# Hashed attention with a mixture of adapters: the shift to the head of each pair, the signs' read ahead of the crossbar transpose, the routing a slot earlier

## The chip, the core and the metric

The program runs on one core of one Trainium2 chip. The metric is device time in microseconds (us) of one execution. The core has five engines with a queue each: TensorE (PE in the profile; PEld is its weight loads), VectorE (DVE), ScalarE (ACT), GpSimd (POOL) and SyncE (SP). SP computes nothing here; it issues nearly all DMAs, in the order in which they are written.

## The reference, cut to what matters

```python
def _attn_ref(q, k, v, proj):            # 4 batches x 8 heads x 768 positions x 64
    q_bits = (np.einsum('bhsd,dk->bhsk', q, proj) > 0).astype(np.int64)   # 6 bits
    k_bits = (np.einsum('bhsd,dk->bhsk', k, proj) > 0).astype(np.int64)
    ...
    mask = q_bucket[:, :, :, None] == k_bucket[:, :, None, :]
    scores = np.where(mask, scale * np.matmul(q, k.transpose(0, 1, 3, 2)), -1000000000.0)
    ...
    return np.matmul(attn, v)            # attn: softmax over keys

def _moe_ref(x, w_gate, A, B):           # x 3072 x 512, 8 experts of rank 16
    logits = x @ w_gate
    topk = np.argpartition(-logits, K, axis=1)[:, :K]          # K = 2
    ...                                  # w: softmax over the two
    return x + sum(w[:, e] * (x @ A[e]) @ B[e])                # over the two chosen
```

A query sees only the keys whose six sign bits are its own. The attention's output goes, batch by batch, through a layer that picks two of eight low-rank adapters for each position.

## The kernel before, in words

The work is cut into 16 pairs of heads (pair p is batch p // 4, heads 2(p % 4) and the next; hp = p % 4). All data of a pair stays on the core. Each pair has nine slots. In slot s TensorE makes a block of 128 x 1024 scores (line 333) into one of three PSUM buffers, ScalarE turns it into weights with one exponential (line 340), two slots behind at most, and TensorE multiplies the weights with v (line 360) into the one bank `pv`, a head at a time; VectorE's `norm` (lines 378 and 380) divides and frees that bank.

The mask is part of the score's product: rows 64 to 70 of `aug` hold the signs of the hash beside the 64 rows of q or k, so that a score is only large where all six signs agree. `aug` has three buffers; that of pair p+2 is made while pair p runs:

- `natcast` (POOL, line 231, two casts) and `cross` (line 237), a DMA through the crossbar that writes q and k transposed, both heads on 128 rows;
- `shift` (line 246), which copies the second head's 64 rows down to rows 0 to 63, queries on VectorE, keys on POOL;
- `turn32` (DVE, line 189), `hash` (PE, line 199, in the bank `m`), `sign` (line 208 on DVE, line 211 on POOL), `sign_out` (line 217), a DMA of the signs to DRAM, and `sign_in` (line 223), a DMA of them back into rows 64 to 71 of `aug`. It overwrites what the crossing left there, so it follows the shift, which reads those rows.

The bank `m` is a single PSUM buffer. Its tenants, in order: the hash, `turn` (x transposed on PE, line 398, copied by DVE, line 399), the logits `lgz` (line 412) until `route2` (lines 441 and 445) has read them, `zt` (line 457) and `delta` (line 465, added to x by DVE, line 475). ScalarE's share in the routing is one small exponential (line 430), which stands between the big ones.

There is no scheduler: the program is recorded as `slot(p, s)` is written, and each engine runs its own instructions in that order. What is written early in a slot stands early in all five queues. SP is a queue like the others: a DMA that waits for its data holds up those behind it.

Of the kernel before, what the change touches and what calls it, by code (L numbers as in the profile page):

```python
# [19 lines left out]
class Emitter:  # L20
# [614 lines left out]
    def moe0(self, p):
        b, hp = p // self.PPB - 1, p % self.PPB
        if b >= 0 and hp == 2:
            self.route2(b, self.G0)
        if 0 <= b < self.B - 2 and hp == 3:
            self.route2(b, self.G1)  # L640
# [30 lines left out]
    def moe_last(self, p, s, b, hp):  # L671
        G0, G1 = self.G0, self.G1
        if hp == 2:
            if s == 2:
# [12 lines left out]
        if hp == 3:
            if s < 5:
                self.delta(b, s + 1)
            if s in (2, 4):  # L690
                self.store(b, s // 2, None, self.nc.sync)
            if s == 0:
                self.store(b, 0, None, self.nc.sync)
            if s == 1:
                self.turn(self.N - 3)
# [165 lines left out]
```

## Time and profile before

| what | value |
|---|---|
| time, median of 2 runs | 204.72 us (204.09 to 205.34) |
| the profiled execution | 207.21 us |
| its span, first to last instruction | 205.4 us |
| mean granted TensorE clock | 0.914 |
| busy: PE, ACT, POOL, DVE | 81%, 71%, 56%, 51% |

The profiled execution is a run of its own, 1.2% above the median of the others; the span is what its trace covers. No engine is busy throughout, so what has to be read is which engine waits for what in each pair.

### The profile page before, as it was taken

The page shows a single profiled execution, that of the slowest core. Times are in us where ns is not written, and L with a number is a line of the kernel's source. Part 1 is how long each engine was busy: PE and PEld are TensorE (multiplying, and loading weights), DVE is VectorE, ACT ScalarE, POOL GpSimd, SP SyncE. Part 2 cuts the span into 40 slices and gives each one's busy share as a digit, 9 for nine tenths or more (in the row PEclk, how much of TensorE's full clock was granted, in tenths as well). Part 3 has the DMA queues.
Part 4 walks back from the last instruction along what each step waited for, and adds up shares of the span by engine and source line. Part 5 has one row for each costly group of instructions (what it writes and reads, how often), then busy time and mean ns, then how long its engine had stood idle before and what let it go on. Part 6 is the DMA issues. An engine that isn't in the chain of part 4 may idle for free.

```text
span 205.4 us, 5316 instructions
## 1 busy us (share of the span) xinstructions
PE 166.1 (81%) x2158; PEld 112.0 (55%) x2159; DVE 105.4 (51%) x310; ACT 146.1 (71%) x168; POOL 115.9 (56%) x174
## 2 busy tenths in 40 slices
PE   7994984697989598989894998989986989698530
PEld 4642653365666366667562676656554767477310
DVE  1474084034253354756764537484946446766560
ACT  2168495368899687979994578899983878976340
POOL 7348489719499919296958055669593343011250
PEclk9999799679799979999999599999997999999975
DMA  5965599774949945747399919694699030142016
GB/s 117 293 131 163 116 333 192 136 202 52 304 73 290 288 82 142 181 107 221 94 279 217 268 23 288 134 258 81 206 213 268 13 112 3 45 167 109 3 62 246
DMA packets 61009, 33.44 MB, mean 163 GB/s; under 512 B 47416, under 2 KB 59192, under 8 KB 60984
## 3 DMA queue, kind: packets, MB, share of 16 engines
q1 hardware_dynamic: 59112, 32.17, 63.2%
q10 hardware_dynamic: 1744, 0.92, 1.5%
q8 instruction: 17, 0.28, 0.6%
q14 instruction: 8, 0.07, 0.1%
q0 software_dynamic: 128, 0.01, 0.0%
HBM read 20.16 MB, written 7.03 MB: 132 GB/s over the span
## 4 chain that ended last, share of the span: by engine, by line
POOL 28%; PE 27%; DMA 16%; issue 13%; DVE 10%; ACT 1%; POOLq 1%; SPq 0%
PE s L333 10%; DMA aug<-dr 9%; PE pv L360 6%; POOL nb L231 5%; POOL vs L179 4%; POOL xb L389 4%; POOL aug L246 4%; POOL vb L177 3%; POOL s L211 3%; DMA vn<-in_v_dram 3%; DVE acc L475 2%; DMA aug<-nb 2%; DMA dr<-s 2%; POOL vs L181 2%; POOL vb L182 2%
## 5 line engine op out<-in xcount | busy, mean ns | idle before, releaser
L340 ACT ACTIVATE P<-s 128x1024 bf16<-128x1024 f32 x144 | 138.5, 1034 | 35.6 <-PE s L333 26.8
L333 PE MATMUL s<-aug 71*128 71x256 bf16 (+2 forms) x384 | 86.7, 335 | 17.2 <-DMA aug<-dr 14.6
L360 PEld LDWEIGHTS <-P 128*128 128x128 bf16 x1080 | 51.5, 103 | 19.0 <-issue 6.9
L360 PE MATMUL pv<-vb,P 128*128 128x65 bf16 x1080 | 54.4, 201 | 0.0
L333 PEld LDWEIGHTS <-aug 71*128 71x128 bf16 x384 | 31.5, 101 | 37.0 <-issue 14.1
L389 POOL CAST xb<-x 128x768 bf16<-128x768 f32 x15 | 13.7, 910 | 58.3 <-DVE x L380 58.2
L189 DVE STREAM_TRANSPOSE R<-nat 128x768 f32<-128x768 f32 x30 | 27.7, 954 | 1.3 <-DMA nat<-in_k_dram 0.9
L231 POOL CAST nb<-nat 128x768 bf16<-128x768 f32 x30 | 24.0, 826 | 1.9 <-DMA nat<-in_q_dram 1.8
L399 DVE COPY xT<-xtp 128x768 bf16<-128x768 bf16 x15 | 8.4, 558 | 26.8 <-PE xtp L398 26.7
L475 DVE SCALAR_TENSOR_TENSOR acc<-dl,rt,x 128x512 f32<-128x512 f32 x21 | 15.6, 748 | 9.3 <-PE dl L465 9.3
L380 DVE TENSOR_TENSOR x<-pv,ri 128x384 f32<-128x384 f32 x30 | 16.7, 557 | 1.0
L179 POOL TENSOR_TENSOR vs<-vn 128x384 f32<-128x384 f32 x16 | 15.9, 995 | 0.0
L211 POOL TENSOR_SCALAR s<-sg,ssc 128x192 bf16<-128x192 bf16 x15 | 11.5, 763 | 5.8 <-DVE sg L208 5.1
L199 PE MATMUL hs<-R,hst 128*32 128x192 f32 x240 | 13.2, 338 | 0.6 <-DVE xT L399 0.6
L346 PE MATMUL pv<-vb,eps 128*128 128x390 bf16 x30 | 11.2, 372 | 3.2 <-POOL vb L182 2.6
L177 POOL CAST vb<-vn 128x768 bf16<-128x768 f32 x16 | 13.3, 830 | 0.6 <-DMA vn<-in_v_dram 0.5
L378 DVE RECIPROCAL ri<-pv 128x6 f32<-128x6 f32 x30 | 5.7, 191 | 15.1 <-PE pv L360 14.7
L246 POOL COPY aug<-aug 64x768 bf16<-64x768 bf16 x15 | 12.5, 830 | 1.7 <-DMA aug<-nb 0.9
L465 PE MATMUL dl<-Bcat,zT 128*128 128x512 bf16 x23 | 8.9, 403 | 3.0 <-DVE acc L475 1.9
L421 DVE MAX8 top<-lz 128x8 f32<-128x8 f32 x24 | 2.7, 163 | 16.1 <-PE lz L412 16.1
L199 PEld LDWEIGHTS hs<-R,hst 128*32 128x32 f32 x240 | 6.5, 111 | 8.0 <-DVE ri L378 2.5
L412 PE MATMUL lz<-wa,xT 128*128 128x136 bf16 x96 | 8.6, 222 | 2.4 <-ACT xT L743 2.1
(83 smaller groups left out, 137.6 us busy)
## 6 DMA issues: line engine op xcount, KB each, us to landing
vn<-in_v_dram SPq DMA_DIRECT2D x16, 384.0 KB, 5.1
nat<-in_q_dram SPq DMA_DIRECT2D x15, 384.0 KB, 5.3
nat<-in_k_dram SPq DMA_DIRECT2D x15, 384.0 KB, 4.9
out_dram<-acc SPq DMA_DIRECT2D x10, 512.0 KB, 3.4
dr<-s SPq DMA_DIRECT2D x15, 48.0 KB, 3.6
aug<-dr SPq DMA_DIRECT2D x15, 48.0 KB
out_dram<-acc SPq DMA_DIRECT2D x2, 256.0 KB, 4.9
out_dram<-acc ACTq DMA_DIRECT2D x1, 512.0 KB
```

Source lines behind the costliest of these rows:

```text
L177: nc.gpsimd.tensor_copy(out=vb[:, :, 0:T, 0:D], in_=vn)
L179: nc.gpsimd.tensor_add(out=s3, in0=vn[:, :, 0:3, :], in1=vn[:, :, 3:6, :])
L189: self.nc.vector.transpose(out=self.R[p][:, i], in_=self.nat[p][:, i])
L199: nc.tensor.matmul(out=self.hs[p][32 * j:32 * j + 32], lhsT=self.hst[:, hf].rearrange("p b i -> p (b i)"), rhs=rhs, start=(hf == 0), stop= ...
L211: nc.gpsimd.tensor_scalar(out=s2, in0=sg, scalar1=self.ssc, scalar2=None, op0=ALU.mult)
L231: self.nc.gpsimd.tensor_copy(out=self.nb[p][:, :, i].rearrange("p t h d -> p h t d"), in_=self.nat[p][:, i].rearrange("p h (t d) -> p h t ...
L246: eng.tensor_copy(out=aug[0:64, :, i, 1, :], in_=aug[64:128, :, i, 0, :])
L333: nc.tensor.matmul(out=ps[:, c - lo:c - lo + n * P], lhsT=aug[0:71, kt, 1, h, :], rhs=aug[0:71, q:q + n, 0, h, :], start=True, stop=True)
L340: self.nc.scalar.activation(out=self.P_[p][:, lo:lo + 1024], in_=ps, func=ACT.Exp, scale=128.0 if p == 0 else 0.125)
L360: self.nc.tensor.matmul(out=pv[:, i, :], lhsT=self.P_[p][:, o:o + P], rhs=vb[:, h, kt, :], start=False, stop=(kt == T - 1), skip_group_che ...
L389: self.nc.gpsimd.tensor_copy(out=self.xb[p], in_=self.x[b][:, :, hp * P:(hp + 1) * P])
L475: nc.vector.scalar_tensor_tensor(out=acc, in0=ps, scalar=rt, in1=x, op0=ALU.mult, op1=ALU.add)
```

## The change

`shift(p+1)` moves from slot 3 or 4 of pair p to its slot 0, on both engines. `sign_in(p+1)` moves from slot 5 to slot 0 and thereby ahead of `cross(p+2)` and of the loads of q and k in SP's queue; only the load of v stays in front of it. The loads of q and k now follow the crossing. The second half of `sign` goes from POOL to VectorE. The logits of a group of three blocks move from slots 6 and 7 to 5 and 6, their exponential from slot 8 to 7, `route2` from the next pair's slot 0 to slot 8. `turn` moves from slots 6, 0, 3, 6 (by hp) to slot 0 of every pair from 2 on. Both `zt` stand in hp 3, four of the six `delta` in slots 5 to 8 of hp 0. The stores of finished rows move from slot 0 to 6. In pair 1 the work for pair 3 stands one slot earlier. At the start there are 21 idle matmuls in three places, in place of 13 in one, and the load of v for pair 1 follows the signs' write.

```diff
@@ sign
-        nc.gpsimd.tensor_scalar(out=s2, in0=sg, scalar1=self.ssc, scalar2=None, op0=ALU.mult)
+        nc.vector.tensor_scalar(out=s2, in0=sg, scalar1=self.ssc, scalar2=None, op0=ALU.mult)
@@ start
-        for i in range(13):
-            nc.tensor.matmul(out=B[:, 0, 0:256], lhsT=self.wz[:, 0:128], rhs=self.wz, start=True, stop=True)
+        def busy(n):
+            for i in range(n):
+                nc.tensor.matmul(out=B[:, 0, 0:256], lhsT=self.wz[:, 0:128], rhs=self.wz, start=True, stop=True)
+
+        busy(16)
         self.T1(0, 0, tm)
         self.tcopy(0, 0, tm, "act")
+        busy(2)
         self.T1(1, 0, tv)
         self.tcopy(1, 0, tv, "act")
+        busy(3)
@@ slot
-        off = 4 if p == 0 else 1 if p == 1 else 0
-        if s == 0:
-            self.moe0(p)
-        if s == 3 + (p == 1) and p and hp < 2:
+        if s == 0 and p:
             self.shift(p + 1)
+        off = 4 if p == 0 else 0
+        if s == 0 and 2 <= p < N:
+            self.turn(p - 2)
         if s - off in (1, 2):
             self.turn32(p + 2, s - off - 1)
...
-        if s == 4 and hp >= 2:
-            self.shift(p + 1)
-        if s - off == 4:
+        late = {0: 8, 1: 5}.get(p, 4)
+        if s == late:
             self.hash(p + 2)
-        if s - off == (4 if p == 0 else 5):
+        if s == min(late + 1, 8):
             self.sign(p + 2)
...
         if s == 0 and p:
-            self.stores(p)
+            self.loadv(p + 2)
+            self.sign_in(p + 1)
+        if s - off == 1:
+            self.cross(p + 2)
+        if s == (6 if p == 0 else 1):
             self.loadqk(p + 3, 0)
             self.loadqk(p + 3, 1)
-            self.loadv(p + 2)
-        if s - off == 1:
-            self.cross(p + 2)
...
-        if s == 5 and p:
-            self.sign_in(p + 1)
-        if s - off == (4 if p == 0 else 5):
+        if s == min(late + 1, 8):
             self.sign_out(p + 2)
+        if s == 6:
+            self.stores(p)
@@ moe
-        if b >= 0 and L and s in (6, 7):
-            for i in (L[0:1], L[1:3])[s - 6]:
+        if L and s in (5, 6):
+            for i in (L[0:1], L[1:3])[s - 5]:
                 self.lgz(b, L, i)
-            if s == 7:
+            if s == 6:
                 self.route1(b, L)
-        if b >= 0 and hp == 3 and s == 5:
-            self.zt(b, G0)
-        if b >= 1 and hp == 0 and s == 2:
-            self.zt(b - 1, G1)
-        D = {(3, 7): 0, (3, 8): 1, (0, 0): 2, (0, 7): 3, (0, 8): 4, (1, 2): 5}.get((hp, s))
+        if L and s == 8:
+            self.route2(b, L)
+        if hp == 3 and s in (5, 6):
+            self.zt(b, (G0, G1)[s - 5])
+        D = {(3, 7): 0, (3, 8): 1, (0, 5): 2, (0, 6): 3, (0, 7): 4, (0, 8): 5}.get((hp, s))
```

In the last two pairs the routing of batch 2 moves likewise: `turn(13)` from slot 1 to slot 0 of pair 15, and `delta(1)` from pair 15 into pair 14.

**SP in pair 8.** Its DMAs before, from the store to the signs' write (the number behind `nat`, `vn`, `nb`, `aug` and `dr` begins with the pair or buffer; `s210` are the signs of pair 10):

```order
L483 DMA out_0_dram<-acc0_0_1684 128x1024
L161 DMA nat11_1716<-in_q_dram 128x2x384
L161 DMA nat11_1716<-in_k_dram 128x2x384
L169 DMA vn10_1719<-in_v_dram 128x2x384
L237 DMA_TRANSPOSE aug1_128<-nb10_1713 128x12x128
L223 DMA aug0_127<-dr9_1645 8x24x128
L217 DMA dr10_1834<-s210_1831 128x6x32
```

The same pair now:

```order
L169 DMA vn10_1735<-in_v_dram 128x2x384
L223 DMA aug0_127<-dr9_1661 8x24x128
L237 DMA_TRANSPOSE aug1_128<-nb10_1733 128x12x128
L161 DMA nat11_1760<-in_q_dram 128x2x384
L161 DMA nat11_1760<-in_k_dram 128x2x384
L217 DMA dr10_1849<-s210_1843 128x6x32
L483 DMA out_0_dram<-acc0_0_1698 128x1024
```

The read of pair 9's signs (line 223) went ahead of the crossing and of two of the three loads; the store went last.

**VectorE in pair 1.** Before, from the signs of pair 2 to the second `norm` of pair 0:

```order
L208 TENSOR_SCALAR sg2_388<-hs2_379 128x192
L378 RECIPROCAL ri0_0_442<-pv0_0_349 128x6
L380 TENSOR_TENSOR x0_440<-pv0_0_349,ri0_0_442 128x6x64
L189 STREAM_TRANSPOSE R3_445<-nat3_334 128x768 x2
L246 COPY aug2_129<-aug2_129 64x6x128
L378 RECIPROCAL ri0_1_510<-pv0_1_460 128x6
```

The same place now:

```order
L208 TENSOR_SCALAR sg2_396<-hs2_387 128x192
L211 TENSOR_SCALAR s22_398<-sg2_396,ssc_203 128x192
L246 COPY aug2_129<-aug2_129 64x6x128
L189 STREAM_TRANSPOSE R3_437<-nat3_342 128x768
L378 RECIPROCAL ri0_0_457<-pv0_0_357 128x6
L380 TENSOR_TENSOR x0_455<-pv0_0_357,ri0_0_457 128x6x64
L189 STREAM_TRANSPOSE R3_437<-nat3_342 128x768
L378 RECIPROCAL ri0_1_519<-pv0_1_472 128x6
```

The shift of pair 2 and the first transpose of pair 3 (which waits for the load `nat3`) now stand ahead of the `norm` of pair 0.

**VectorE from the end of pair 8 to the head of pair 9.** Before (`dl0_4` and `dl0_5` are two of the deltas of batch 0, `xtp7` is x of pair 7 transposed):

```order
L475 SCALAR_TENSOR_TENSOR acc0_2_1887<-dl0_4_1885,rt0_3_1523,x0_440 128x512
L378 RECIPROCAL ri8_0_1897<-pv8_0_1815 128x6
L380 TENSOR_TENSOR x2_1895<-pv8_0_1815,ri8_0_1897 128x6x64
L399 COPY xT1_1115<-xtp7_1900 128x768
L189 STREAM_TRANSPOSE R11_1934<-nat11_1716 128x768 x2
L475 SCALAR_TENSOR_TENSOR acc0_2_1887<-dl0_5_1956,rt0_3_1523,x0_440 128x512
L246 COPY aug1_128<-aug1_128 64x6x128
```

Now:

```order
L475 SCALAR_TENSOR_TENSOR acc0_1_1847<-dl0_2_1845,rt0_0_1319,x0_455 128x512
L475 SCALAR_TENSOR_TENSOR acc0_1_1847<-dl0_3_1868,rt0_3_1522,x0_455 128x512
L475 SCALAR_TENSOR_TENSOR acc0_2_1884<-dl0_4_1882,rt0_3_1522,x0_455 128x512
L475 SCALAR_TENSOR_TENSOR acc0_2_1884<-dl0_5_1897,rt0_3_1522,x0_455 128x512
L378 RECIPROCAL ri8_0_1908<-pv8_0_1827 128x6
L380 TENSOR_TENSOR x2_1906<-pv8_0_1827,ri8_0_1908 128x6x64
L246 COPY aug1_128<-aug1_128 64x6x128
L399 COPY xT1_1123<-xtp7_1913 128x768
L189 STREAM_TRANSPOSE R11_1944<-nat11_1760 128x768 x2
```

Four deltas now stand in a row in pair 8, and the shift stands ahead of the copy of xT and of the transposes.

## Rows read from the trace of the kernel before

**Rows 1.** Waits: engine, line, waited for; us in total, times, longest.

```profile
ACT P L340 <- PE s L333: 26.8, 35, 5.0
PE s L333 <- DMA aug<-dr: 14.6, 8, 4.7
```

**Rows 2.** Timeline of ACT: start, us, instruction, idle before and its releaser.

```profile
38.74 1.94 ACT L340 ACTIVATE P<-s 128x1024 bf16<-128x1024 f32 x2 [5.02 <-PE s L333]
...
113.39 1.02 ACT L340 ACTIVATE P<-s 128x1024 bf16<-128x1024 f32 x1 [3.33 <-PE s L333]
...
124.22 0.22 ACT L430 ACTIVATE e<-d 128x24 f32<-128x24 f32 x1 [1.24 <-DVE d L423]
...
180.69 2.05 ACT L340 ACTIVATE P<-s 128x1024 bf16<-128x1024 f32 x2 [1.29 <-PE s L333]
```

**Rows 3.** Windows by pairs: length; PE, PEld, DVE, ACT, POOL busy; clock; DMA; GB/s.

```profile
24.49:38.74 14.25, 8.94 (x132) 5.73 (x129) 6.86 (x12) 8.61 (x9) 13.29 (x18) 0.94 1.05 219
38.74:60.74 22.00, 19.90 (x242) 13.53 (x241) 7.68 (x17) 17.68 (x18) 13.05 (x22) 0.80 0.68 161
60.74:82.45 21.71, 18.52 (x261) 12.80 (x260) 10.16 (x33) 17.30 (x20) 16.33 (x24) 0.92 0.82 203
...
100.61:126.16 25.55, 21.77 (x267) 14.32 (x267) 14.54 (x41) 18.06 (x19) 14.56 (x21) 0.87 0.86 208
126.16:144.33 18.17, 17.04 (x255) 11.78 (x252) 11.37 (x34) 16.81 (x21) 12.24 (x16) 1.00 0.70 166
144.33:168.10 23.77, 20.19 (x267) 13.39 (x267) 14.43 (x40) 17.94 (x19) 12.98 (x19) 0.93 0.74 175
168.10:189.42 21.32, 18.41 (x296) 14.41 (x292) 12.81 (x44) 17.56 (x21) 3.11 (x5) 1.00 0.20 78
```

**Rows 4.** Timeline at the head of pair 9, SP and PE.

```profile
106.72 0.35 SPq L223 DMA_DIRECT2D aug<-dr  x1
...
112.26 1.03 PE L333 MATMUL s<-aug 71*128 71x512 bf16 x3 [2.48 <-DMA aug<-dr]
```

**Rows 5.** Chain that ended last: start, us, what.

```profile
12.13 4.09 DMA aug<-nb
...
47.37 2.45 DMA aug<-dr
...
106.72 5.50 DMA aug<-dr
```

**Rows 6.** Tile `aug`: crossing's issue and the shift, ns min/median/max; the DMAs' landing.

```profile
L237 SPq DMA_TRANSPOSE aug<-nb x15: 1426/2692/3422, 12.1 to 154.0; - x15
...
L246 DVE COPY aug<-aug x15: 356/356/721, 16.2 to 171.9; 64x768 bf16<-64x768 bf16 x15
L246 POOL COPY aug<-aug x15: 821/826/923, 16.4 to 173.0; 64x768 bf16<-64x768 bf16 x15
...
DMA to landing us min/median/max: 6.0/7.0/8.0
```

**Rows 7.** The page's costliest groups: busy us, mean ns of one, idle before.

```profile
L231 POOL CAST nb<-nat 128x768 bf16<-128x768 f32 x30 | 24.0, 826 | 1.9 <-DMA nat<-in_q_dram 1.8
...
L380 DVE TENSOR_TENSOR x<-pv,ri 128x384 f32<-128x384 f32 x30 | 16.7, 557 | 1.0
```

**Rows 8.** The page's DMA issues: KB each, median us to landing.

```profile
dr<-s SPq DMA_DIRECT2D x15, 48.0 KB, 3.6
```

**Rows 9.** Timeline of pair 1, PE and DVE.

```profile
26.76 0.34 PE L346 MATMUL pv<-vb,eps 128*128 128x390 bf16 x1 [0.45 <-DVE x L380]
...
26.99 2.03 DVE L189 STREAM_TRANSPOSE R<-nat 128x768 f32<-128x768 f32 x2 [0.29 <-DMA nat<-in_q_dram]
```

**Rows 10.** Timeline of PE in pair 12, the third of three deltas.

```profile
144.64 0.38 PE L465 MATMUL dl<-Bcat,zT 128*128 128x512 bf16 x1 [0.41 <-DVE acc L475]
```

**Rows 11.** Timeline of PE at the start.

```profile
1.04 2.95 PE L505 MATMUL hb<-wz 128*128 128x256 bf16 x13 [1.04 <-DVE wz L71]
...
5.93 2.93 PE L274 MATMUL ha<-qkT,projW 128*128 128x384 f32 x4
```

More of the change, by code (lines that the diff above doesn't have):

```diff
@@ L531, in first @@
             self.loadqk(2, 1)
-            self.loadv(1)
             self.cast(0, 1)
@@ L542, in first @@
             self.sign_out(1)
+            self.loadv(1)
             self.sign_here(0, 1, self.hc)
@@ L575, in slot @@
             self.norm(p - 1, 0)
-        off = 4 if p == 0 else 1 if p == 1 else 0
-        if s == 0:
-            self.moe0(p)
-        if s == 3 + (p == 1) and p and hp < 2:
+        if s == 0 and p:
             self.shift(p + 1)
+        off = 4 if p == 0 else 0
+        if s == 0 and 2 <= p < N:
+            self.turn(p - 2)
         if s - off in (1, 2):
             self.turn32(p + 2, s - off - 1)
-        if s == 4 + (p == 1):
+        if s == (5 if p == 1 else 4):
             self.norm(p - 1, 1)
             self.to_bf(p - 1)
-        if s == 4 and hp >= 2:
-            self.shift(p + 1)
-        if s - off == 4:
+        late = {0: 8, 1: 5}.get(p, 4)
+        if s == late:
             self.hash(p + 2)
-        if s - off == (4 if p == 0 else 5):
+        if s == min(late + 1, 8):
             self.sign(p + 2)
@@ L601, in slot @@
         if s == 0 and p:
-            self.stores(p)
+            self.loadv(p + 2)
[3 more added lines that the diff above has]
+        if s == (6 if p == 0 else 1):
             self.loadqk(p + 3, 0)
             self.loadqk(p + 3, 1)
-            self.loadv(p + 2)
-        if s - off == 1:
-            self.cross(p + 2)
         if p == 0 and s == 6:
-            self.loadqk(3, 0)
-            self.loadqk(3, 1)
             self.loadv(2)
-        if s == 5 and p:
-            self.sign_in(p + 1)
-        if s - off == (4 if p == 0 else 5):
+        if s == min(late + 1, 8):
             self.sign_out(p + 2)
+        if s == 6:
+            self.stores(p)
         if p in (1, 2, 3) and s in (6, 7):
@@ L626, in route_exps @@
             return
-        if s == 8 and hp == 1:
+        if s == 7 and hp == 1:
             self.route_exp(b, self.G0)
         if b == self.B - 2:
-            if hp == 2 and s == 6:
+            if hp == 2 and s == 4:
                 self.route_exp(b, self.G1)
-        elif s == 8 and hp == 2:
+        elif s == 7 and hp == 2:
             self.route_exp(b, self.G1)
[L635 to L640, printed above, removed]
     def stores(self, p):
@@ L650, in moe @@
         G0, G1 = self.G0, self.G1
-        if p < self.N - 1 and s == (6, 0, 3, 6)[hp] and p >= 2:
-            self.turn(p - 2)
+        if b < 0:
+            return
         if b == self.B - 2 and hp >= 2:
@@ L655, in moe @@
         L = {1: G0, 2: G1}.get(hp)
-        if b >= 0 and L and s in (6, 7):
-            for i in (L[0:1], L[1:3])[s - 6]:
+        if L and s in (5, 6):
+            for i in (L[0:1], L[1:3])[s - 5]:
                 self.lgz(b, L, i)
-            if s == 7:
+            if s == 6:
                 self.route1(b, L)
-        if b >= 0 and hp == 3 and s == 5:
-            self.zt(b, G0)
-        if b >= 1 and hp == 0 and s == 2:
-            self.zt(b - 1, G1)
-        D = {(3, 7): 0, (3, 8): 1, (0, 0): 2, (0, 7): 3, (0, 8): 4, (1, 2): 5}.get((hp, s))
-        if hp < 2:
+        if L and s == 8:
[3 more added lines that the diff above has]
+        D = {(3, 7): 0, (3, 8): 1, (0, 5): 2, (0, 6): 3, (0, 7): 4, (0, 8): 5}.get((hp, s))
+        if hp == 0:
             b -= 1
@@ L673, in moe_last @@
         if hp == 2:
-            if s == 2:
+            if s == 1:
                 self.zt(b, G0)
-            if s in (4, 5):
-                for i in (G1[0:2], G1[2:3])[s - 4]:
+            if s in (2, 3):
+                for i in (G1[0:2], G1[2:3])[s - 2]:
                     self.lgz(b, G1, i)
+            if s == 3:
+                self.route1(b, G1)
             if s == 5:
-                self.route1(b, G1)
+                self.route2(b, G1)
             if s == 6:
-                self.route2(b, G1)
-            if s == 7:
                 self.zt(b, G1)
-            if s == 8:
-                self.delta(b, 0)
+            if s in (7, 8):
+                self.delta(b, s - 7)
         if hp == 3:
-            if s < 5:
+            if s in (1, 2, 3, 4):
                 self.delta(b, s + 1)
[L690 to L695, printed above, removed]
+            if s in (0, 3, 5):
+                self.store(b, (0, 3, 5).index(s), None, self.nc.sync)
     def pv3(self, u, parts, where=None):
```

## The prediction

> **What bounds the kernel now.** I read the waits first. ScalarE's exponentials are the one long, even stream (144 of them), and they waited 26.8 us for scores; TensorE in turn waited 14.6 us, eight times, for the DMA that brings a pair's signs into `aug` [rows 1]. ACT's timeline then says where: the gaps sit at the heads of pairs, 5.02 us ahead of pair 2, 3.33 us ahead of pair 9, and shorter ones of the same kind ahead of pairs 5 and 13 [rows 2]. The windows, two pairs each, show what such a gap costs in all. Pairs 10 and 11 have none: 18.17 us, clock 1.00, PE busy 17.0 and ACT 16.8 of them (pairs 6 and 7 repeat it). Pairs 2 and 3, 4 and 5, 8 and 9, 12 and 13 have one each: 22.00, 21.71, 25.55 and 23.77 us, at a granted clock of 0.80 to 0.93 [rows 3]. So a gap is paid twice: while TensorE stands, and behind it, when part of the stretch runs at 1.2 instead of 2.4 GHz and PE, already as full as ACT, cannot keep up. A pair without a gap is bound by PE and ACT together, near 9.1 us.
>
> Why the signs are late can be read at pair 9. SP issues the read at 106.72, late in pair 8, and the read takes 5.50 us to land because crossing and loads are in front of it; TensorE starts the pair at 112.26, after 2.48 us of standing [rows 4, 5]. With little in front, a read lands 2.45 us after its issue [rows 5].
>
> **The read's new place (the main term).** The shift of pair p+1 now needs only its crossing, issued in slot 1 of the pair before, and the read follows right behind the shift, about 1.2 us into the pair (a `norm` and a copy on VectorE). Even at 5.50 us it is there at 6.7, before the 9.1 us are over; at 2.45 us there are some 5 us to spare. The gap goes, unless the read cannot be issued: it waits for its own signs' write. That is a loop through SP: read's issue 0.35 us [rows 4], crossing's issue 2.69 [rows 6], the issue of two loads (I put 0.65 each, nearly twice the read's), the signs' write 3.6 to landing [rows 8]: 7.9 us a pair, under 9.1. A second loop goes through POOL: crossing, shift 0.83 [rows 6], two casts of 0.83 [rows 7], next crossing. The crossing took 4.09 us early in the program [rows 5] and 6.0 to 8.0 behind loads [rows 6]. Now the loads come after it, so I take a value near 4.09: 6.6 us a pair; with 7.0 it would be 9.5. Both loops fit, the second not at all values.
>
> What is late next is then PE and ACT themselves, that is, the quiet pairs' time. Two pairs without routing (2 and 3) lack one wait of the routing, 1.24 us [rows 2], against 18.2, and I leave them some 0.5 for the first crossings: 17.5, a gain of 4.5. Pairs 4 and 5: 18.2, a gain of 3.5. Pairs 8 and 9, 12 and 13 also carry the deltas, below.
>
> **Deltas in a row.** Each delta and each `turn` wants the single bank `m` when VectorE has just been given it; the third of three deltas waited 0.41 us for the one before [rows 10]. Four deltas now stand in slots 5 to 8 of hp 0, and the `turn` of hp 1 behind them: four such waits, 1.6 us, on a PE that has nothing to spare. Pairs 8 and 9, and 12 and 13: 18.2 + 1.6 = 19.8, gains of 5.7 and 4.0. The bounds are 0 (if ACT's two slots of lead hide the waits) and 3.2.
>
> **Pair 1.** The gap of 5.02 us at its end goes: the signs of pair 2 need no shift late in pair 1 any more, and their read is not behind pair 3's crossing. But here the change adds a wait. VectorE's `norm` of pair 0, which frees the bank `pv`, now stands behind the first transpose of pair 3, and that waits for a load which landed at 26.99 [rows 9]. Queued behind it on VectorE is the `norm`, and TensorE waits for that with all of pair 1 behind it. TensorE had the bank at 26.76, after 0.45 us of waiting [rows 9]; now a transpose (half of 2.03 us) and a `norm` (0.56 [rows 7] and its short reciprocal, some 0.75) lie between 26.99 and its start: about 28.75, 2.0 us later. Whether so long a stand lowers the clock is open; after the stands of pairs 2, 5, 9 and 13 it did [rows 3], so I add 0.9, bounds 0 and 1.7. Pair 1 gains 5.0 - 2.0 - 0.9 = 2.1.
>
> **Routing, and the last pairs.** Logits, exponential and `route2` move by the same slot, so ACT's wait of 1.24 us for the logits [rows 2] stays: the hash still lies just ahead of them on PE. I cost it at nothing, bounds -0.6 and +0.3 for each of six. In pair 15 a delta and the `turn` cost ACT 1.29 us [rows 2]; one delta goes to pair 14 (0.4 there): a gain of 0.9.
>
> **The start.** Eight more idle matmuls. The 13 took 2.95 us, 0.21 each from start to start [rows 11]; the three added ahead end before the first transposes can start, the five between are at worst 1.1 us on the path. The four hash matmuls took 2.93 us at 1.2 GHz [rows 11]; if the fuller engine gets its clock before them, they take half, and 0.5 to 1 is won. I take 0.
>
> **POOL to VectorE.** 15 multiplications of some 0.36 us, the row of VectorE's copy [rows 6]; VectorE is busy 11.4 of 18.2 us in the quiet pairs [rows 3], and nobody waits for signs within a pair. 0, and 5.4 with no cover.
>
> **The sum** against the profiled execution: 2.1 + 4.5 + 3.5 + 5.7 + 4.0 + 0.9 = 20.7 of 205.4 us of span, so 184.7; the same off the median of 204.72 gives **184.0 us**. With the bounds of the terms, 180 to 190.
>
> **The rivals.**
>
> *The crossing still lands late (0.10).* For it: seven microseconds is its median [rows 6]. Then POOL and VectorE, which now have the shift first in a pair, stand at the head of every pair until it lands. At 8.0 a pair takes 8.0 + 0.83 + 1.66 = 10.5; fourteen of them 147, against 132 in my sum (17.5 + 18.2 x 3 + 19.8 x 2 + 20.4): 199. Against it: the 8.0 were behind three loads and a store.
>
> *Slower: the read misses every pair's start (0.05).* The read waits in SP for its signs' write, which now lies behind two loads that lie behind the crossing. With 3.42 us for the crossing's issue and 5.5 us for the write instead of 3.6, the loop is 0.35 + 3.42 + 1.3 + 5.5 = 10.6, over the 9.1 from which it decides. Before, four heads stood; now fourteen would, each at what pairs 4 and 5 paid, 3.5: 184 + 49 = 233.
>
> *The first pairs do not follow (0.12).* Pairs 1 to 3 depend on the first loads, at a DMA share of 1.05 of the engines' time in pair 1 [rows 3], not on the order. Without 2.1 and 4.5: 190.6.
>
> *The two halves of the shift hold each other up (0.03).* They now run side by side at each head. One copy of 15 on VectorE took 0.72 us instead of 0.36 [rows 6]; in its timeline a cast of POOL runs beside it. If each shift and no cover: 15 x 0.36 = 5.4, so 189.4. The Trainium skill, SBUF — State Buffer, "Who interferes with whom", says so in general: a VectorE copy in a two-port mode and a GpSimd instruction shut each other out for the whole of whichever began first. By that rule the one late copy is no accident, and the shift would last 0.36 + 0.83 at worst. The row agrees in part (0.72, not 1.19).
>
> *Better (0.10).* The deltas' waits are hidden (3.2) and half of the routing's waits go (3.7): 177.
>
> **How the numbers follow.** My forecast has 0.60, and 184.0 is its time. A measurement of this kernel can tell about 2% (200.6 to 208.8) from no change. Faster takes in the forecast, the first-pairs rival, the shift rival, the better one and half of the late crossing: 0.60 + 0.12 + 0.03 + 0.10 + 0.04 = 0.89; same is the rest of the late crossing, 0.06; slower 0.05. From 177 to 197 only the slower rival, half of the late crossings and half of the better case stay out, 0.15.
>
> **What the profile would show.** Right: no wait of TensorE for `aug<-dr` from pair 3 on, granted clock 1.00 from pair 4 to 15, quiet pairs of 18 us in all windows, PE waiting near 0.4 us for `acc` in hp 0, a stand of about 2.4 us for the `norm` in pair 1, ACT still waiting 1.2 us for the logits. Wrong: VectorE or POOL idle at pairs' heads for `aug<-nb`, SP waiting long for `dr<-s`, or a new wait of PE for the bank `m` that lasts over a microsecond and takes the clock with it.

## The result, and the profile after

The changed kernel takes 187.44 us (187.00 and 187.89, two runs) against 204.72: a ratio of 0.916, interval 0.900 to 0.931. Run again beside the kernel before, it took 185.77 us (183.61 to 187.44, six runs), ratio 0.909 (0.902 to 0.916). The prediction was 184.0, range 177 to 197. The profiled execution took 187.89 us, its span is 186.1 us, its mean granted clock 0.951. The profiled executions of the changed kernel and of runs 1, 2, 5 and 6 are the longest of their kernels' runs and that of run 4 is the shortest of its, so their rows are read for the place of a wait and not for a total.

The waits of the changed kernel (engine, line, waited for; us in total, times, longest):

```profile
POOL aug L246 <- DMA aug<-nb: 22.5, 13, 5.0
...
ACT P L340 <- PE s L333: 10.9, 23, 2.5
ACT e L430 <- DVE d L423: 10.1, 9, 1.8
...
PE pv L346 <- POOL vb L182: 4.3, 1, 4.3
```

TensorE's wait for `aug<-dr`, 14.6 us before [rows 1], has no row any more, and ScalarE waits 10.9 instead of 26.8 us. POOL now stands 22.5 us for the crossing, in front of its half of the shift, and only the first of these stands, 5.03 us, has a wait of TensorE behind it (below).

Its windows: pair 0, pair 1, then two pairs each, cut at the first exponential of a pair as in [rows 3]:

```profile
9.00:24.89 15.89, 10.62 (x129) 5.60 (x124) 6.85 (x12) 8.78 (x10) 10.14 (x15) 0.89 0.59 149
24.89:38.03 13.14, 11.04 (x138) 7.09 (x135) 5.30 (x11) 8.61 (x9) 8.49 (x11) 0.74 0.85 227
38.03:54.84 16.81, 16.79 (x245) 11.25 (x243) 11.04 (x23) 16.62 (x19) 11.72 (x20) 1.00 1.05 210
54.84:72.56 17.72, 17.08 (x259) 11.99 (x257) 11.71 (x36) 16.75 (x21) 13.41 (x20) 1.00 1.07 234
72.56:90.17 17.61, 16.73 (x252) 11.68 (x249) 12.24 (x35) 16.64 (x20) 12.30 (x17) 1.00 0.74 192
90.17:111.54 21.37, 19.55 (x270) 13.16 (x270) 16.18 (x43) 17.74 (x20) 12.66 (x18) 1.00 0.83 205
111.54:129.15 17.61, 16.73 (x252) 11.68 (x249) 11.92 (x35) 16.64 (x21) 11.71 (x16) 1.00 0.90 225
129.15:150.08 20.93, 19.17 (x270) 12.99 (x270) 15.63 (x43) 17.74 (x20) 13.22 (x19) 1.00 0.71 155
150.08:170.06 19.98, 17.87 (x290) 14.14 (x286) 12.10 (x42) 17.48 (x21) 2.26 (x5) 1.00 0.28 109
```

The clock, the third number from the end, is 1.00 in all pairs from 2 to 15. Pair 1 has 0.74: the only stretch at half clock that costs much now lies there. The gains by stretch, against [rows 3] and the starts of the exponentials in the two traces:

| stretch | before | after | gain | predicted |
|---|---|---|---|---|
| to the first exponential | 10.61 | 9.00 | 1.6 | 0 |
| pair 0 | 13.88 | 15.89 | -2.0 | 0 |
| pair 1 | 14.25 | 13.14 | 1.1 | 2.1 |
| pairs 2, 3 | 22.00 | 16.81 | 5.2 | 4.5 |
| pairs 4, 5 | 21.71 | 17.72 | 4.0 | 3.5 |
| pairs 6, 7 and 10, 11 | 36.3 | 35.22 | 1.1 | 0 |
| pairs 8, 9 | 25.55 | 21.37 | 4.2 | 5.7 |
| pairs 12, 13 | 23.77 | 20.93 | 2.8 | 4.0 |
| pairs 14, 15 | 21.32 | 19.98 | 1.3 | 0.9 |
| sum of the span | | | 19.3 | 20.7 |

Three places are left where time stands. The first two are in pairs 0 and 1; PE's timeline there (start, us, instruction, idle before and its releaser):

```profile
20.49 0.33 PE L346 MATMUL pv<-vb,eps 128*128 128x390 bf16 x1 [4.25 <-POOL vb L182]
...
28.81 0.51 PE L346 MATMUL pv<-vb,eps 128*128 128x390 bf16 x1 [2.10 <-DVE x L380]
```

What is in front of the two releasers on their engines, POOL and VectorE:

```profile
16.60 0.92 POOL L246 COPY aug<-aug 64x768 bf16<-64x768 bf16 x1 [5.03 <-DMA aug<-nb]
17.59 0.83 POOL L177 CAST vb<-vn 128x768 bf16<-128x768 f32 x1
```

```profile
27.11 0.98 DVE L189 STREAM_TRANSPOSE R<-nat 128x768 f32<-128x768 f32 x1 [0.99 <-DMA nat<-in_q_dram]
28.20 0.56 DVE L380 TENSOR_TENSOR x<-pv,ri 128x384 f32<-128x384 f32 x1
```

POOL stands 5.03 us in the shift of pair 1, with the cast of v for pair 0 behind it. VectorE waits for a load of pair 3 with the `norm` of pair 0 behind it. Both are stands of the order: what the engine waits for is not what TensorE needs. The third place is the row of deltas in pair 8, read from ACT's timeline:

```profile
97.82 1.02 ACT L340 ACTIVATE P<-s 128x1024 bf16<-128x1024 f32 x1 [0.19 <-PE s L333]
99.04 1.02 ACT L340 ACTIVATE P<-s 128x1024 bf16<-128x1024 f32 x1 [0.20 <-PE s L333]
100.32 1.02 ACT L340 ACTIVATE P<-s 128x1024 bf16<-128x1024 f32 x1 [0.26 <-PE s L333]
...
108.70 0.22 ACT L430 ACTIVATE e<-d 128x24 f32<-128x24 f32 x1 [1.60 <-DVE d L423]
```

The exponentials start 1.22 to 1.28 us apart there, against 0.91 in a quiet pair (8.19 us for nine in pair 7). The last row is the wait for the logits, which stays as it was.

### The profile page after: what moved, and what is told of

Same layout as the page of the kernel before. It is cut to its first block, busy times and chain, and to the rows that moved or that the text cites. A ratio compares the mean times of both kernels' runs of the same rounds, so it can differ in the third digit from the quotient of the medians.

```text
span 186.1 us, 5336 instructions
## 1 busy us (share of the span) xinstructions
PE 157.9 (85%) x2166; PEld 107.3 (58%) x2167; DVE 112.9 (61%) x325; ACT 143.6 (77%) x168; POOL 105.7 (57%) x159
## 4 chain that ended last, share of the span: by engine, by line
PE 29%; DMA 27%; POOL 16%; ACT 11%; DVE 6%; issue 5%; SPq 2%; POOLq 1%
DMA nat<-in_q_dram 17%; PE s L333 10%; ACT P L340 10%; DMA aug<-nb 9%; POOL nb L231 7%; PE pv L360 7%; PE hs L199 3%; POOL vs L179 3%; POOL vb L177 3%; DVE acc L475 2%; SPq L237 2%; PE dl L465 2%; DMA nat<-in_k_dram 2%; PE lz L412 2%; PE xtp L398 2%
## 5 line engine op out<-in xcount | busy, mean ns | idle before, releaser
L340 ACT ACTIVATE P<-s 128x1024 bf16<-128x1024 f32 x144 | 136.1, 1054 | 19.3 <-PE s L333 10.9
L333 PE MATMUL s<-aug 71*128 71x256 bf16 (+2 forms) x384 | 82.1, 320 | 2.9 <-ACT P L340 2.8
L360 PEld LDWEIGHTS <-P 128*128 128x128 bf16 x1080 | 48.0, 99 | 18.1 <-issue 5.6
L360 PE MATMUL pv<-vb,P 128*128 128x65 bf16 x1080 | 51.1, 196 | 0.0
L231 POOL CAST nb<-nat 128x768 bf16<-128x768 f32 x30 | 24.9, 831 | 11.2 <-DMA nat<-in_q_dram 7.9
L246 POOL COPY aug<-aug 64x768 bf16<-64x768 bf16 x15 | 12.6, 837 | 24.9 <-DMA aug<-nb 22.5
L389 POOL CAST xb<-x 128x768 bf16<-128x768 f32 x15 | 12.3, 822 | 23.4 <-DVE x L380 23.4
L346 PE MATMUL pv<-vb,eps 128*128 128x390 bf16 x30 | 10.2, 339 | 6.8 <-POOL vb L182 4.3
L199 PE MATMUL hs<-R,hst 128*32 128x192 f32 x240 | 15.9, 359 | 0.1
L208 DVE TENSOR_SCALAR sg<-hs 128x192 bf16<-128x192 f32 x15 | 5.4, 358 | 12.9 <-PE hs L199 12.9
L246 DVE COPY aug<-aug 64x768 bf16<-64x768 bf16 x15 | 8.5, 567 | 3.7 <-DMA aug<-nb 3.2
```

The source lines that it names most:

```text
L199: nc.tensor.matmul(out=self.hs[p][32 * j:32 * j + 32], lhsT=self.hst[:, hf].rearrange("p b i -> p (b i)"), rhs=rhs, start=(hf == 0), stop= ...
L231: self.nc.gpsimd.tensor_copy(out=self.nb[p][:, :, i].rearrange("p t h d -> p h t d"), in_=self.nat[p][:, i].rearrange("p h (t d) -> p h t ...
L246: eng.tensor_copy(out=aug[0:64, :, i, 1, :], in_=aug[64:128, :, i, 0, :])
L333: nc.tensor.matmul(out=ps[:, c - lo:c - lo + n * P], lhsT=aug[0:71, kt, 1, h, :], rhs=aug[0:71, q:q + n, 0, h, :], start=True, stop=True)
L340: self.nc.scalar.activation(out=self.P_[p][:, lo:lo + 1024], in_=ps, func=ACT.Exp, scale=128.0 if p == 0 else 0.125)
L360: self.nc.tensor.matmul(out=pv[:, i, :], lhsT=self.P_[p][:, o:o + P], rhs=vb[:, h, kt, :], start=False, stop=(kt == T - 1), skip_group_che ...
```

## The experiments

Each kernel was timed beside the kernel before on its chip; a ratio is to that.

**Run 1: the shift and the signs' read alone**, on the kernel before.

```diff
-        if s == 3 + (p == 1) and p and hp < 2:
+        if s == 0 and p:
             self.shift(p + 1)
...
         if s == 0 and p:
             self.stores(p)
-            self.loadqk(p + 3, 0)
-            self.loadqk(p + 3, 1)
             self.loadv(p + 2)
+            self.sign_in(p + 1)
         if s - off == 1:
             self.cross(p + 2)
+        if s == (6 if p == 0 else 1 + off):
+            self.loadqk(p + 3, 0)
+            self.loadqk(p + 3, 1)
...
-        if s == 5 and p:
-            self.sign_in(p + 1)
```

> The kernel before, with only the shift at slot 0, the load of v and the signs' read right behind it, and the loads of q and k behind the crossing; pair 1's old offset, routing, start, stores and POOL's multiplication stay. Theory (the read's place in the queue makes nearly the whole gain): pairs 2 to 5 lose their 9 us and pairs 8, 9, 12 and 13 some 5 to 7 of the gaps and the slow clock behind them, 189 to 193 us, PE waits under 2 us in all for aug<-dr. Rival (the routing's new places carry the gain of pairs 8, 9, 12 and 13): 196 to 199, with gaps left in those pairs.

Measured: 190.87 us, ratio 0.938 (0.930 to 0.946). Its windows of pair 1, of pairs 2 and 3, 4 and 5, and 8 and 9:

```profile
24.34:33.29 8.95, 8.30 (x133) 5.49 (x129) 4.97 (x10) 8.58 (x10) 8.51 (x13) 1.00 0.83 232
33.29:52.87 19.58, 16.53 (x242) 10.92 (x241) 9.37 (x19) 17.04 (x19) 15.86 (x25) 1.00 1.02 181
52.87:72.97 20.10, 17.83 (x261) 12.05 (x260) 10.68 (x26) 17.15 (x20) 15.21 (x21) 1.00 1.06 231
...
91.60:112.65 21.05, 18.72 (x268) 12.52 (x267) 14.41 (x32) 17.90 (x20) 13.04 (x19) 1.00 0.95 249
```

As the theory has it: the clock is 1.00 in all four, and PE's waits for `aug<-dr` are down to a single one of 0.5 us. What was not expected is pair 1: 8.95 us, against 13.14 in the changed kernel. Here pair 1 still has its old offset, and the `norm` stands ahead of the transposes. Pairs 2 to 5, from which the theory expected 9 us, gave 2.4 and 1.6; with the 5.3 of pair 1 that is 9.3, where the changed kernel's pairs 1 to 5 gave 10.3. Behind the early start of pair 2 VectorE waits for loads (1.06, 1.49 and 0.78 us ahead of its transposes in pairs 2 to 4), and TensorE's hash waits behind it, 1.71 us at the longest.

**Run 2: the routing alone**, on the kernel before (`turn` at slot 0, logits, exponential, `route2`, `zt` and deltas as in the change).

> The kernel before, with only the routing moved: logits in slots 5 and 6, exponential in 7, route2 in 8, turn in slot 0, both zt in hp 3, four deltas in hp 0. Theory (the signs' read decides): 203 to 206 us, PE still waits some 14 us for aug<-dr, the clock near 0.91. Rival (the routing carries part of the gain): 195 to 200.

Measured: 200.11 us (196.43 to 202.84), ratio 0.974 (0.959 to 0.988). PE's waits of it:

```profile
PE s L333 <- DMA aug<-dr: 12.8, 6, 4.1
```

Neither end is met. The gaps stay, as the theory says, but the routing is worth some 2.6% by itself, with a wide interval. The two parts together, 0.938 x 0.974 = 0.913, make the whole of 0.909 to 0.916: they add up. Some 70% of the gain is the signs' and 30% the routing's, as far as the interval of run 2 allows.

**Run 3: the read back at slot 5**, on the changed kernel; the shift stays first.

```diff
         if s == 0 and p:
             self.loadv(p + 2)
-            self.sign_in(p + 1)
...
+        if s == 5 and p:
+            self.sign_in(p + 1)
         if s == min(late + 1, 8):
             self.sign_out(p + 2)
```

> The changed kernel, with the signs' read put back to slot 5, behind crossing and loads; the shift stays in slot 0. Theory (the read's place in SP's queue decides): gaps come back at several heads and the clock falls behind them, 195 to 203 us, PE waits 5 to 15 us for aug<-dr. Rival (the shift's place decides, since the read had waited for a late shift): 187 to 189, no wait of PE for aug<-dr beyond 1 us.

Measured: 191.61 us, ratio 0.939 (0.929 to 0.950), between the two theories. PE's wait, and the windows of pairs 2 and 3 and of pairs 5 and 6, in which the clock is below 1.00:

```profile
PE s L333 <- DMA aug<-dr: 3.9, 2, 3.0
```

```profile
37.54:56.49 18.95, 18.04 (x245) 12.45 (x243) 10.06 (x20) 16.94 (x19) 11.42 (x19) 0.87 0.79 176
65.77:86.86 21.09, 19.98 (x277) 14.14 (x275) 13.79 (x49) 17.29 (x20) 15.44 (x21) 0.92 0.70 172
```

The two waits are 3.03 us ahead of pair 2 and 0.91 ahead of pair 4. Ahead of pair 5 TensorE stands 1.45 us:

```profile
55.78 0.59 PE L333 MATMUL s<-aug 71*128 71x512 bf16 x3 [0.91 <-DMA aug<-dr]
...
65.08 0.60 PE L333 MATMUL s<-aug 71*128 71x512 bf16 x3 [1.45 <-ACT P L340]
```

The second row names ScalarE. The read for pair 5 went out at 60.44, 4.6 us before TensorE went on, about what the other two late reads took (4.6 and 5.2 us), so that the signs are the likelier cause; the trace does not show it. The clock falls behind the stands of pairs 2 and 5. Two or three gaps come back, then, of eight waits before. In pair 8 none does. SP's timeline there, whose pair begins at 95.05:

```profile
93.24 2.02 SPq L237 DMA_TRANSPOSE aug<-nb  x1
...
96.74 0.30 SPq L223 DMA_DIRECT2D aug<-dr  x1
```

The read goes out 1.7 us into the pair, although it is written in slot 5: SP knows no slots, and had begun to issue the crossing before the pair began. The same place before the change, SP and VectorE, in the pair that begins at 100.61:

```profile
103.30 3.24 SPq L237 DMA_TRANSPOSE aug<-nb  x1
```

```profile
104.24 0.36 DVE L246 COPY aug<-aug 64x768 bf16<-64x768 bf16 x1
```

There the shift was through at 104.60, 4.0 us into the pair, and the read went out at 106.72 [rows 4], once the crossing's issue was over. In run 3 the two come early: the shift stands first, and the crossing no longer behind the loads. The read's own place in the queue costs where the crossing and the loads in front of it go out late: the reads for pairs 2, 4 and 5 were issued 7.6, 2.3 and 4.0 us into the pair before. These three have the shortest lead, 5.3 to 5.9 us before their pair's first exponential; the others had 6.1 or more. Of the whole gain the read's place carries 5 to 6 us (0.939 against 0.909 to 0.916).

**Run 4: the old 13 idle matmuls**, on the changed kernel.

```diff
-        busy(16)
+        busy(13)
...
-        busy(2)
...
-        busy(3)
```

> The changed kernel, with the old 13 idle matmuls in one place instead of 21 in three. Theory (the fuller engine got its clock before the hash matmuls, and the start won 1.6 us): first exponential 1.6 us later, 188.5 to 189.5 us. Rival (what the start won is given back in pair 0, where TensorE waits for vb, which does not depend on the start): first exponential later, pair 0 shorter by as much, 187.0 to 187.8.

Measured: 186.57 us, ratio 0.917 (0.912 to 0.923), the changed kernel's own time. The first exponential came at 9.31, not 1.6 us later. PE's timeline has the reason, the four hash matmuls at full clock, first in this run:

```profile
6.06 1.53 PE L274 MATMUL ha<-qkT,projW 128*128 128x384 f32 x4
```

and in run 1, with the same 13 idle matmuls in the same place:

```profile
6.04 2.90 PE L274 MATMUL ha<-qkT,projW 128*128 128x384 f32 x4
```

So this trace did not start late, and the run tests the theory's total and not its step. 13 sometimes get the clock before the hash and sometimes do not: the first exponential came at 9.31, 10.61, 10.67 and 10.77 in the four traces with 13, and at 8.90 to 10.00 in the ten with 21. The added matmuls may make the early rise likelier, but the theory falls, since the time is the same: what an early start brings is lost in pair 0, as the rival has it: pair 1 begins at 24.34 to 24.77 in the three traces that started late, and at 23.41 to 25.49 in the eight that started early with the same order on POOL.

**Run 5: the changed kernel again.**

> The changed kernel itself, beside the kernel before on the same chip, as the base for what follows: 186.5 to 188 us, ratio 0.912 to 0.920. If the phase of the start decides (one run of the 13 idle matmuls had its clock at 5.7 us, three at 9.7 to 10.2), its runs spread over some 2 us.

Measured: 185.77 us (183.61 to 187.44), ratio 0.909 (0.902 to 0.916). The median lies below the expected 186.5 to 188, and the spread is 3.8 us, wider than expected: differences between the runs below of under 1% tell nothing.

**Run 6: the `norm` ahead in pair 1.**

```diff
-        if s - off in (1, 2):
-            self.turn32(p + 2, s - off - 1)
+        lag = 1 if p == 1 else off
+        if s - lag in (1, 2):
+            self.turn32(p + 2, s - lag - 1)
```

> The changed kernel, with both transposes of pair 3 one slot later in pair 1, so that the norm of pair 0 stands ahead of them on VectorE. Theory (the norm behind the first transpose is what pair 1 loses): the stand of 2.1 us and the half clock behind it go, pair 1 takes 9 to 10.5 us in place of 13.2, 183.5 to 185.5 us. Rival (pair 1 is held by the loads, and the stand moves to another wait, for the signs of pair 2): 186.5 to 188.

Measured: 184.63 us, ratio 0.906 (0.901 to 0.911). The windows of pair 1 and of pairs 2 and 3:

```profile
25.49:34.35 8.86, 8.41 (x139) 5.76 (x137) 5.27 (x11) 8.56 (x10) 6.06 (x8) 0.99 0.81 229
34.35:52.31 17.96, 16.83 (x246) 11.32 (x244) 10.27 (x22) 16.53 (x19) 13.33 (x21) 1.00 1.02 225
```

Pair 1 falls from 13.14 to 8.86 us with its clock at 0.99; pairs 2 and 3 give 1.1 back, as the hash of pair 4 stands 1.13 us for its transposes. But 13.14 is not the rule: without this edit pair 1 took 10.70, 10.03 and 9.97 us in the traces of runs 4, 8 and 11, with stands of 2.40, 1.74 and 1.68 us for the `norm` and the clock at 1.00. In run 4:

```profile
27.91 0.34 PE L346 MATMUL pv<-vb,eps 128*128 128x390 bf16 x1 [2.40 <-DVE x L380]
```

```profile
23.69:34.39 10.70, 8.30 (x138) 5.75 (x135) 5.02 (x12) 8.58 (x9) 6.83 (x9) 1.00 0.85 236
```

In the whole it is a gain of some 1 us that the intervals do not part from none.

**Run 7: the cast of v first.**

```diff
+            self.vcast(0)
             self.shift(1)
             self.sign_in(1)
-            self.vcast(0)
```

> The changed kernel, with the cast of v of pair 0 ahead of the shift of pair 1 on POOL, which stood 5.03 us for the crossing with that cast behind it. Theory (POOL's stand in front of the cast makes pair 0 long): TensorE's wait of 4.25 us for vb goes, pair 0 takes 12 to 13.5 us in place of 15.9, 183.5 to 186 us. Rival (v lands as late as the crossing, or pair 1's signs then come late by what the cast takes): pair 0 or pair 1 longer by 2 to 3 us elsewhere, 186.5 to 189.

Measured: 183.83 us, ratio 0.905 (0.899 to 0.911). Pair 0:

```profile
9.01:20.91 11.90, 9.59 (x129) 5.16 (x125) 7.67 (x12) 8.67 (x9) 9.49 (x14) 1.00 0.77 188
```

Pair 0 falls by 4.0 us, as the theory says (by 2.2 to 4.6 against the other traces with the old order); pair 1 keeps its stand, 2.58 us, and takes 12.39. The total is 1.0% under run 5's, which the intervals do not part.

**Run 8: the routing's exponential a slot later.**

```diff
-        if s == 7 and hp == 1:
+        if s == (7 if p == self.N - 3 else 8) and hp == 1:
...
-            if hp == 2 and s == 4:
+            if hp == 2 and s == 5:
...
-        elif s == 7 and hp == 2:
+        elif s == 8 and hp == 2:
...
-        if s == 0 and 2 <= p < N:
+        if s == (3 if hp >= 2 and 4 < p < N - 2 else 0) and 2 <= p < N:
             self.turn(p - 2)
```

> The changed kernel, with the routing's exponential one slot later (8 instead of 7 in hp 1 and 2, 5 instead of 4 in pair 14; pair 13 as it was), and the turn of hp 2 and 3 in slot 3, as the bank comes free later. Theory (ScalarE stands some 1.0 us for the logits with the next big exponential already possible): four waits of 0.96 to 1.6 us go, 183.5 to 185.5 us. Rival (PE and ACT are both full there, so that ACT's wait is taken from a wait it has anyway, or the hash stands for the bank): 186.5 to 188.

Measured: 187.29 us, ratio 0.916 (0.908 to 0.923). Its waits:

```profile
ACT e L430 <- DVE d L423: 6.3, 8, 1.8
PE pv L346 <- DVE x L380: 3.9, 6, 1.7
```

ACT's wait falls by 3.8 us and nothing is won. `route2`, which stands on VectorE in front of the next pair's `norm`, now gets its exponential later, and TensorE waits 0.41 us for that `norm` at the heads of pairs 6, 7, 10 and 11. The pair with the logits gets shorter (pair 5 takes 8.91 us instead of 9.58) and the one after the routing longer (pair 7 9.28 instead of 8.19).

**Run 9: both edits to the first pairs** (runs 6 and 7 together).

> The changed kernel, with both edits to the first pairs: the cast of v of pair 0 ahead of the shift of pair 1, and the norm of pair 0 ahead of pair 3's transposes. Theory (two separate stands of the order, 4 us in pair 0 and 3 to 4 us in pair 1): pair 0 near 12, pair 1 near 9, pair 2 begins near 30, 180 to 182 us. Rival (the first loads hold these pairs, and what one edit saves stands again at the next head, as pair 2 took 9.8 in place of 8.6 with the norm alone): 183 to 185.

Measured: 182.25 us, ratio 0.898 (0.890 to 0.906). Pairs 0, 1, and 2 and 3:

```profile
9.40:20.91 11.51, 9.27 (x129) 5.18 (x126) 7.45 (x12) 8.67 (x9) 9.44 (x14) 1.00 0.79 186
20.91:30.07 9.16, 8.45 (x133) 5.49 (x130) 5.14 (x11) 8.55 (x9) 6.48 (x9) 1.00 0.83 229
30.07:48.54 18.47, 17.21 (x249) 11.60 (x250) 10.03 (x21) 16.84 (x19) 13.29 (x21) 1.00 1.03 216
```

The clock is at 1.00 throughout, pair 2 begins at 30.07 instead of 38.03. Of these 8 us pairs 2 and 3 give 1.7 back: the hash of pair 4 stands 0.92 us for transposes, which wait for their loads. The 8 us are against one trace; in runs 11 and 12 pair 2 begins at 35.33 and 35.62. Beside it on the same chip, runs 11 and 12, which have the changed kernel's first pairs, took 186.12 and 185.40 us: this version is 1.7 to 2.1% faster than they are.

**Run 10: run 9 with the deltas spread.**

```diff
-        D = {(3, 7): 0, (3, 8): 1, (0, 5): 2, (0, 6): 3, (0, 7): 4, (0, 8): 5}.get((hp, s))
-        if hp == 0:
+        D = {(3, 7): 0, (3, 8): 1, (0, 2): 2, (0, 6): 3, (0, 8): 4, (1, 2): 5}.get((hp, s))
+        if hp < 2:
             b -= 1
```

> As the run before, and four deltas spread: slots 2, 6 and 8 of hp 0 and slot 2 of hp 1 in place of 5 to 8 of hp 0. Theory (the loop of delta and acc through the one bank, 1.22 us a turn, is longer than a slot of 0.9, and costs 0.3 in each of five slots in a row): pairs 8 and 9, 12 and 13 take 1 to 1.5 us less each two, 177.5 to 180 us. Rival (PE is as full there with the deltas' own work, and a delta in hp 1 delays the hash or the logits): within 1 us of the run before.

Measured: 181.80 us, ratio 0.896 (0.891 to 0.901): the rival. It has the lowest median of all, but is not told apart from run 9.

**Run 11: the deltas spread, on the changed kernel** (the diff of run 10).

> The changed kernel, with the deltas spread alone (slots 2, 6 and 8 of hp 0, slot 2 of hp 1). Theory (the four in a row cost 1 to 1.5 us for each batch): 183 to 184.5 us, PE's waits for acc fall from 3.3 to under 2 us. Rival (no more is lost by it than by any place of the deltas): 185.5 to 187.

Measured: 186.12 us, ratio 0.916 (0.909 to 0.922): the rival again. PE's waits for `acc`, and the window of pairs 8 and 9:

```profile
PE hs L199 <- DVE acc L475: 2.6, 4, 0.9
PE xtp L398 <- DVE acc L475: 2.0, 5, 0.4
PE dl L465 <- DVE acc L475: 1.1, 4, 0.4
```

```profile
87.74:109.61 21.87, 18.79 (x270) 12.79 (x270) 16.57 (x43) 17.61 (x21) 13.74 (x19) 1.00 0.79 203
```

The waits did not fall, they moved to the hash, which is the next tenant of the bank: 5.7 us in the three rows, against 3.3 in the changed kernel (1.7 for `dl`, 1.6 for `xtp`). The pairs take 21.87 us, no less than the 21.37 with four in a row.

**Run 12: the second half of the sign back on POOL**, on the changed kernel.

```diff
-        nc.vector.tensor_scalar(out=s2, in0=sg, scalar1=self.ssc, scalar2=None, op0=ALU.mult)
+        nc.gpsimd.tensor_scalar(out=s2, in0=sg, scalar1=self.ssc, scalar2=None, op0=ALU.mult)
```

> The changed kernel, with the second half of the sign back on POOL. Theory (its place costs and brings nothing, since nobody waits for signs within a pair): 185.5 to 187.5 us. Rival (on POOL it holds up the casts and the next shift's chain, 15 times some 0.4 us; or, the other way, VectorE is relieved where it is full with acc and norm): 188 to 191, or 183 to 184.5.

Measured: 185.40 us, ratio 0.913 (0.907 to 0.920). No difference.

## Why the prediction was right, point by point

**What bounds the kernel.** Right: a gap was paid twice, and with the gaps the half clock went, to 1.00 from pair 2 on. Pairs 2 and 3 gave 5.2 us for 4.5 predicted, pairs 4 and 5 4.0 for 3.5. Run 1, which moves the shift and the read alone, got 9.3 of the 10.3 us of pairs 1 to 5, but 5.3 of them in pair 1: how this gain divides among the first pairs is not the read's doing alone, and that each stretch came near its own term is in part luck.

**The read's new place.** The time was right, the cause only in part. The read goes out early, 1.5 us into pair 8, where 1.2 was predicted, and in front of the crossing. SP's timeline:

```profile
91.67 0.30 SPq L223 DMA_DIRECT2D aug<-dr  x1
92.08 1.42 SPq L237 DMA_TRANSPOSE aug<-nb  x1
```

The prediction laid the lateness to the crossing and loads in front of the read. For pair 9 that holds for 2.1 us of the 6.1 (the crossing's issue after the shift was through); the other 4.0 were the shift's late place. Run 3 shows that with the shift and the crossing early the read's place decides at the heads of two or three pairs alone. The shift's place by itself, with the old order of crossing and loads, was not tried. The loop through SP was over-priced: the crossing's issue took 1.43 us in the median and not 2.69 [rows 6]. Tile `aug` (ns min/median/max):

```profile
L237 SPq DMA_TRANSPOSE aug<-nb x15: 1273/1432/1803, 11.0 to 141.3; - x15
L246 DVE COPY aug<-aug x15: 355/513/1007, 16.5 to 149.4; 64x768 bf16<-64x768 bf16 x15
```

**Quiet pairs.** I put them at 18.2 and left 6, 7, 10 and 11 at no gain; they came to 17.6. Run 2, which moves the routing alone, has them shorter too (9.42 and 8.18 us for pairs 10 and 11, as in the changed kernel), run 1 does not (18.49): it is the routing's new places.

**Deltas in a row: mis-sized.** 19.8 was predicted for pairs 8 and 9; they took 21.37 (pairs 12 and 13: 20.93). The term added four waits to a quiet stretch and left out the time of the work itself on a full PE: the quiet pairs 10 and 11 hold two deltas, these hold four. PE is busy 19.55 us there, against 16.73 in pairs 6 and 7, and idle 1.82 against 0.88. Of the 2.82 us of work two more deltas of 0.38 [rows 10] are 0.8, and two more runs of transposes for `turn` that fall into the window, of 0.49 each, are 1.0; the rest I cannot assign. The waits of `xtp` and `dl` there come to 1.2 us (0.8 and 0.4), not 1.6, and run 11 shows that to spread the deltas wins none of it.

**Pair 1: mis-sized.** The stand for the `norm` was 2.10 us in the trace, 2.0 more predicted; TensorE started at 28.81, 28.75 predicted. The half clock behind it was put at 0.9. With the stand gone pair 1 takes 8.9 to 9.2 us (runs 1, 6, 9 and 10), with the stand and the clock at 1.00 10.0 to 10.7 (runs 4, 8 and 11), with the stand and the clock at 0.74 13.1 (here and in run 5). So the stand cost 0.8 to 1.8 us, and the half clock, where it came, 2.4 to 3.2 and not 0.9, which is beyond the bound of 1.7.

**The start and pair 0: a step that was missing.** I took the start at 0 with a possible gain. It gained 1.6 us, pair 0 lost 2.0, and the prediction has no term for pair 0. TensorE cannot get `vb` before POOL is through the shift of pair 1 and the cast behind it: it had it at 19.3 to 20.6 us, whether the first exponential came at 8.90 (20.58) or at 10.00 (19.70). Run 7 takes that away and wins 4.0 in pair 0. The eight added matmuls themselves bought nothing that can be measured (run 4).

**The routing's wait** stayed, 0.75 to 1.60 us each, as predicted, and run 8 shows that it is not free to take. **POOL to VectorE** cost nothing (run 12). **Pairs 14 and 15** gained 1.3 for 0.9.

**The rivals.** The crossing took 3.8 to 5.6 us from its issue until POOL went on, in the 13 heads where POOL waited for it; the sum has 4.09, and the 6.0 to 8.0 of [rows 6] are two landings. With 5.6 the loop through POOL is 8.1 us, under the 9.1, and no wait of TensorE but that of pair 0 hangs on it. Two signs that the prediction names for its being wrong did come: POOL idle for `aug<-nb`, and SP waiting for the signs' write:

```profile
SPq L223 <- DMA dr<-s: 29.3, 12, 3.8
```

After pair 0 neither reached TensorE, since SP issues each read 6.6 to 9.4 us before the pair that needs it (91.67 for 100.32 in pair 8), and so the slower rival did not come near. The rival of the first pairs falls with the 5.2 us of pairs 2 and 3.

The rival of the two shift halves has the wrong partner. VectorE's half took 0.513 us in the median and 1.007 at most, against 0.356 before [rows 6], but the halves seldom run side by side: POOL runs ahead and made its half for pair 10 at 97.23, VectorE at 101.30. Where they did run together, at 16.48 and 25.76, VectorE's took 0.355. What held it up was mostly another instruction of POOL, here the product for `vs`:

```profile
101.30 0.96 DVE L246 COPY aug<-aug 64x768 bf16<-64x768 bf16 x1
```

```profile
101.05 1.00 POOL L179 TENSOR_TENSOR vs<-vn 128x384 f32<-128x384 f32 x1
```

The Trainium skill, SBUF — State Buffer, "Who interferes with whom", makes such an overlap a lock for the whole of the first. The trace agrees: ten of the 15 copies lasted longer than 0.36 us, each had an instruction of POOL running when it began, and each ended 0.20 to 0.22 us after that instruction did. Over 15 shifts it is 3.2 us on VectorE (8.5 against 15 x 0.356), and no wait of TensorE names the shift.

**The sum.** 187.44 us, and 185.77 when run again, lie near 184.0 partly because terms missed both ways: the start 1.6, pairs 2 to 5 1.2, the quiet pairs 1.1 and the last two 0.4 for the better, the deltas 2.7, pair 0 2.0 and pair 1 1.0 for the worse. In the chances half of the late crossing is 0.04 in one place and 0.05 in another; nothing hangs on it.

## What to carry to other kernels

Look behind the instruction that waits, on its own engine: POOL's stands for the crossing left the later pairs at their quiet time and cost some 4 us in the one pair where the next instruction in its queue was on TensorE's path. In a DMA queue that runs ahead of the engines, what holds a DMA is the data it waits for and the issue of those in front; the slot in which it is written says less: in run 3 a read written in slot 5 went out 1.7 us into pair 8, though over all pairs its place was worth 5 to 6 us. And price work that is moved into a full stretch at its own duration as well as by its waits.

## What the runs showed of the hardware that was not expected

The same 13 idle matmuls from 1.05 to 4.0 us left the four hash matmuls at half clock in the kernel before and in run 1 (2.93 and 2.90 us) and at full clock in run 4 (1.53). The engine had done the same before in all of them. The Trainium skill, TensorE: Matmul & The Clock Gate, "Part 1: The HAM clock gate (the "warmup" mystery)", says that the moment of the rise differs from run to run of one kernel. These traces agree, and by more than the half microsecond that it gives: the clock rose at 5.7 us in run 4 and at 9.7 to 10.2 in the other three that start with 13.

Nor does the length of a stand tell by itself whether the clock falls. In pair 1 of the changed kernel it fell to 1.2 GHz with a stand of 2.10 us (0.74 over the pair), and in run 3 behind one of 1.45 us (0.92 over pairs 5 and 6); in run 4 it stayed at 2.4 GHz through one of 2.40 us at the same place (1.00 over pair 1).

The issue of the crossbar transpose costs SP less in the changed kernel, where the loads of q and k follow it: 1.43 us in the median in place of 2.69, with the same 15 transposes of the same shape. It goes with the place of the loads: 1.43 in run 1, which puts them behind the crossing, and 2.56 in run 2, which leaves them in front. Why is not shown.
